# Fetching the odd heads' rows of w_in through a second DMA queue, and two of its pieces earlier

## The chip, the cores and the metric

The kernel runs on one core of a Trainium2 chip. A core has TensorE (matmuls), VectorE, ScalarE and GpSimd (elementwise work), and SyncE, which here only issues DMAs. ScalarE can issue DMAs too; each of the two has a queue of its own. The engines run their instruction lists in order and wait for each other through semaphores. The metric is the time of one execution on the device in microseconds (us), as the median over runs.

## The reference

A DeltaNet attention block feeds a SiLU feed-forward block. q, k, v and the output are float32; the two weights arrive as 64-bit numbers.

```
# q, k, v: (4, 8, 768, 48) float32, beta: (4, 8, 768)
k_n = k / (norm(k) + 1e-6)
state = zeros(B, H, 48, 48)
for t in range(768):
    y[t]  = q[t] @ state
    v_old = state^T @ k_n[t]
    state = state + beta[t] * outer(k_n[t], v[t] - v_old)
x = y as (B*S, H*D) = (3072, 384)
h = x @ w_in                      # w_in (384, 2048)
out = (h * sigmoid(h)) @ w_out    # w_out (2048, 384)
```

## The kernel before

The sequence is cut into 6 chunks of 128 tokens; a chunk has 4 units, one per batch. For each chunk the recurrence is turned into matrix form: `turn` transposes k and q through TensorE (tile `pt`) and copies them to `kq`; `score` makes the masked products `pa` into `ap`; `block_out` and `block_in` carry the 32 x 32 diagonal blocks through a DRAM tile so that all of them lie side by side in `g`; `invert` inverts them by 30 rank-one steps on VectorE (lines 477 and 481, tiles `rank` and `x`) and writes the inverses to DRAM as `up` and `low` (line 492); `move` (line 502) reads them back as `xi` and `xe` (in chunk 0 `xe` lies in `sums_of_w[1]`). `solve` then does the substitution: `merge` joins the 32-blocks (tiles `py`, `px`, line 551), `inner` and `across` apply them to v (tile `pz`), `update` and `new` make the new state and the output, whose transpose is `xT`. `feed_forward` of a chunk (`hidden` with tile `phid`, then `project` or `combine`) is spread between the steps of the next chunk's attention.

Weights arrive as 64-bit numbers and are narrowed to float32 on the chip. w_in comes in 8 pieces of 256 columns (`fetch_w_in`), w_out in 8 pieces of two 128-row blocks (`fetch_w_out`). A raw piece is 768 KB. A raw piece of w_in lands over 128 partitions by four DMAs, listed in `ROWS` (line 150): even heads fill partitions 0 to 63 (48 rows and 16 rows), odd heads 64 to 127 (48 and 16). The raw pieces live in rooms that are free at the time: pieces 0 to 3 in w_out's own buffers, 4 to 6 in buffers of the tag `gT`, 7 in `sums_of_g`. `narrow` (line 157) is five elementwise steps per piece: two on ScalarE (165, 170), three on VectorE (167, 173, 177), one addition on GpSimd (181). `fill(n)` takes the next n of these steps from `queue`, in the order of the pieces, and puts them between the steps of the attention; `Piece.begin` issues a piece's first ScalarE step.

The order is written out by hand. `pin` chains the instructions of an engine in program order; `in_line` does it for DMAs. All DMAs are issued by SyncE. The framework gives DMAs eight semaphores in turn, so each DMA's issue waits until the eighth DMA before it has landed. Where the DMA in question is issued by an engine that computes too, the wait stands in that engine's list.

In chunk 0, which the change touches, the order is: k and q of chunk 0, w_in pieces 0 and 1, blocks out and in, k of chunk 1, w_in pieces 2 and 3, q of chunk 1, v of chunk 0 (lines 914 to 954), the inversion, w_in pieces 4 to 7 and w_out piece 0 (lines 965 to 967), w_out piece 1, and in the substitution w_out pieces 2, 3, 4 and 5. During the inversion's steps 3, 5, 7 and 9 the four units of chunk 1 are transposed (line 960). `busy` (line 273, tile `pw`) puts filler products on TensorE; 20 of them stand after step 18 of the inversion (line 962) and some between the substitution's steps (line 996).

Of the kernel before, what the change touches and what calls it, by code (L numbers as in the profile page):

```python
# [21 lines left out]
def kernel(  # L22
# [22 lines left out]
    nc = tc.nc  # L45
    B, H, S, D = q.shape
# [7 lines left out]
    W = 64  # L54
# [24 lines left out]
    def behind(later, earlier, how=NoSync):  # L79

        tc.add_manual_dep(
            later.ins, earlier.ins.name,
            mybir.DependencyInfo(how, mybir.DependencyReason.DATA), reason="order",
        )
# [3 lines left out]
    def pin(op):  # L88

        engine = op.ins.engine  # L90
        if engine in pins:
            behind(op, pins[engine])
        pins[engine] = op
        return op
# [3 lines left out]
    def in_line(dma):  # L98

        if line:  # L100
            behind(dma, line[-1])
        line.append(dma)
        return dma
# [11 lines left out]
    def packed(t):  # L115
        return t[:].rearrange("p a e w -> p (a e) w")[:, :, 0:D]

    def chunk_of(src, i):
        b, c = units[i]
        return src[b, :, c * C : (c + 1) * C, :].rearrange("h t d -> t h d")  # L120

    def load_k(i):
        if i < N:
            in_line(nc.sync.dma_start(out=packed(kbufs[i % NK]), in_=chunk_of(k, i)))

    def load_q(i):
        if i < N:
            in_line(nc.sync.dma_start(out=packed(zbufs[i % NZ]), in_=chunk_of(q, i)))

    def load_v(i):  # L130
        if i < N and i not in vfs:
            vfs[i] = load.tile([P, H, D], FP32, name="vf", bufs=4)
            in_line(nc.sync.dma_start(out=vfs[i][:], in_=chunk_of(v, i)))
# [9 lines left out]
    for load_one in (load_k, load_q):  # L143
        for i in range(B):
            load_one(i)
    w_in = const.tile([P, NKT, DFF], FP32, name="w_in")
    HFF = NFF // 2
# [1 line left out]

    ROWS = [  # L150
        (at, lambda a, e=e, n=n: (2 * a + e) * D if n == D else (6 + e) * D + a * (W - D), n)
        for e in range(2)
        for at, n in ((W * e, D), (W * e + D, W - D))
    ]
    w_outs = [const.tile([P, HFF, DM], FP32, name=f"w_out{i}") for i in range(2)]

    def narrow(to, raw):

        low, high = raw[..., 0], raw[..., 1]
        bits = to.bitcast(U32)
        pin(nc.scalar.activation(out=to, in_=high.bitcast(FP32), func=ACTF.Abs))
        yield
        yield pin(nc.vector.tensor_scalar(
            out=to, in0=to, scalar1=LOW_HIGH, scalar2=None, op0=ALU.max
        ))
        pin(nc.scalar.activation(  # L170
            out=low.bitcast(I32), in_=low, func=ACTF.Identity, scale=2.0**-29, bias=plus23[:]
        ))
        yield pin(nc.vector.tensor_scalar(
            out=bits, in0=bits, scalar1=3, scalar2=0x3FFFFFFF,
            op0=ALU.logical_shift_left, op1=ALU.bitwise_and,
        ))
        done = pin(nc.vector.scalar_tensor_tensor(
            out=bits, in0=high, scalar=0xC0000000, in1=bits,
            op0=ALU.bitwise_and, op1=ALU.bitwise_or,
        ))  # L180
        adds.append(pin(nc.gpsimd.tensor_tensor(  # L181
            out=to.bitcast(I32), in0=to.bitcast(I32), in1=low.bitcast(I32), op=ALU.add
        )))
        yield done
# [5 lines left out]
    WF = GT  # L190
    NWI = DFF // WF
# [3 lines left out]
    def room(i, k):  # L195
        flat = w_outs[i][:].rearrange("p f m -> p (f m)").bitcast(U32)
        return flat[:, k * SIZE : (k + 1) * SIZE]

    def fetch_w_in(i):
        if i < 4:  # L200
            raw = room(1 - i // 2, i % 2)
        elif i < NWI - 1:
            raw = mlp.tile([P, SIZE], U32, name="raw", tag="gT", bufs=3)[:]
        else:
            raw = spare
        raw = raw.rearrange("p (a f) -> p a f", a=NKT)
        for at, row, rows in ROWS:
            step = row(1) - row(0)
            src = moe_w_in[row(0) : row(0) + rows, i * WF : (i + 1) * WF].bitcast(U32)
            pitch = src.ap[0][0]  # L210
            src = bass.AP(
                tensor=src.tensor, offset=src.offset,
                ap=[[pitch, rows], [pitch * step, NKT], [1, 2 * WF]],
            )
            in_line(nc.sync.dma_start(out=raw[at : at + rows], in_=src))
        raws[i] = raw.rearrange("p a (f j) -> p a f j", j=2)

    raws = {}

    sums_of_g = const.tile([P, 2, NFF // 2, C], FP32, name="sums_of_g")  # L220
    spare = sums_of_g[:].rearrange("p k f t -> p (k f t)").bitcast(U32)[:, 0:SIZE]
# [2 lines left out]
    sums_of_w = [const.tile([P, NFF // 2, HM], FP32, name=f"sums_of_w{i}") for i in range(3)]  # L224

    def narrow_w_in(i):
        return narrow(w_in[:, :, i * WF : (i + 1) * WF], raws.pop(i))

    places = {}

    def fetch_w_out(i):
        if i in (0, 1, 5):
            raw = room(1, min(i, 1))
        elif i in (4, 7):
            raw = sums_of_w[2 if i == 4 else 0][:].rearrange("p f m -> p (f m)").bitcast(U32)
        elif i == 6:
            raw = spare
        else:
            k = int(i == 3)
            if k not in places:  # L240
                places[k] = work.tile([P, SIZE], U32, name="raw_out", tag="ap", bufs=4)
            raw = places[k][:]
        raw = raw.rearrange("p (a f) -> p a f", a=2)
        src = moe_w_out.rearrange("(a p) f -> p a f", p=P)[:, 2 * i : 2 * i + 2, :].bitcast(U32)
        in_line(nc.sync.dma_start(out=raw, in_=src))
        raws[i] = raw.rearrange("p a (f j) -> p a f j", j=2)

    def narrow_w_out(i):
        at = 2 * i % HFF
        return narrow(w_outs[2 * i // HFF][:, at : at + 2, :], raws.pop(i))  # L250


    ident = const.tile([P, P], FP32, name="ident")
# [3 lines left out]
    for t in bkbufs:  # L257
# [4 lines left out]
        out=above[:], in_=above[:], pattern=[[1, P]], compare_op=ALU.is_gt, fill=0.0,  # L262
# [25 lines left out]
    def beta_of(c):  # L288
        pb = bank(psA, "a", "pb")
        pin(nc.tensor.transpose(pb[:, 0:BH], beta_fm[:, c * C : (c + 1) * C], ident[0:BH, 0:BH]))  # L290
        pin(nc.scalar.activation(out=beta_tok[:, c, :], in_=pb[:, 0:BH], func=ACTF.Copy))
# [51 lines left out]
    sizes, steps = {}, {}  # L343
# [524 lines left out]
                yield from project(c, b, o)  # L868


    A, CC, M = (psA, "a"), (psC, "c"), (psM, "m")

    def go(steps, n=1):
# [39 lines left out]
        scale(b)  # L913
    for i in range(B, 2 * B):
        load_k(i)
    fetch_w_in(2)
    fetch_w_in(3)
    for i in range(B, 2 * B):
        load_q(i)
    queue, narrowed = deque(), []  # L920

    class Piece:
        def __init__(self, name, steps):
            self.name, self.steps, self.begun, self.done = name, steps, False, 0

        def begin(self):
            if not self.begun:
                next(self.steps)
                self.begun = True

    def fill(n):

        ops = []
        while len(ops) < n and queue:
            piece = queue[0]
            piece.begin()

            if len(queue) > 1 and piece.done >= 2 and piece.name != ("out", 5):
                queue[1].begin()
            ops.append(next(piece.steps))  # L940
            piece.done += 1
            if piece.done == 3:
                narrowed.append(piece.name)
                queue.popleft()
        return ops


    queue.extend(Piece(("in", i), narrow_w_in(i)) for i in range(2))
    fill(5)
    for _ in range(4):  # L950
        busy()

    for i in range(B):
        load_v(i)
    next_us = []
    for n, done in enumerate(invert(0)):
        if n == 1:
            for c in range(1, NCH):
                beta_of(c)
        if n in (3, 5, 7, 9):  # L960
            next_us.append(list(turn(B + len(next_us), M, M))[0])
        if n == 18:
            for i in range(20):
                busy(done if i == 0 else None, Sync)
    for i in range(4, NWI):
        fetch_w_in(i)
    fetch_w_out(0)
    squares(1)
    norms(1)
    queue.extend(Piece(("in", i), narrow_w_in(i)) for i in range(2, NWI))  # L970
    queue.append(Piece(("out", 0), narrow_w_out(0)))

    def until(piece):
        while piece is not None and piece not in narrowed:
            fill(1)
# [1 line left out]
    def more(i, behind=None):  # L977

        until(behind)
        fetch_w_out(i)  # L980
        queue.append(Piece(("out", i), narrow_w_out(i)))

    fill(3)
    for b in range(B):
        size(b)
    more(1, ("in", 1))
    pieces = feed_forward(0)
    for n, _ in enumerate(solve(0, us)):
        fill(2)
        if n == 3:  # L990
            more(2)
            more(3)
            more(4)
        if n == 8:
            more(5, ("out", 1))
        for _ in range((3, 3, 2, 2, 1, 1, 1)[n] if n < 7 else 0):
            busy()
        if n >= 7:
            go(pieces, 2)
# [35 lines left out]
    for c in range(1, NCH):  # L1035
        if c + 1 < NCH:
# [7 lines left out]
            n = 0  # L1044
# [46 lines left out]
```

## Time and profile before

| what | us |
|---|---|
| median of 3 runs | 770.54 (770.52 to 770.78) |
| the profiled execution | 770.21 |
| its span | 768.5 |
| TensorE busy | 730.4 (95% of the span) |
| VectorE busy | 411.8 (54%) |
| ScalarE busy | 233.3 (30%) |
| GpSimd busy | 83.6 (11%) |
| DMA queue q1, share of 16 engines | 31.1% |

The span reaches from the first to the last instruction. Rows of the profile name an engine (PE is TensorE, PEld its weight loads, DVE VectorE, ACT ScalarE, POOL GpSimd, SP SyncE, SPq what SyncE issues), a line of the kernel, an operation, and output<-input. Where the page cuts the span in 40 slices, one slice is 19.2 us and a digit is the busy share in tenths. The chain that ended last is followed back from the last instruction; each of its rows gives a start, a duration and what was running or being waited for. A row "issue" is time in which the engine waited for nothing that the profile shows. DMA rows at SPq give the time of issuing, not of moving.

### The profile page before, as it was taken

To read this page: it belongs to the slowest core of one execution; us is meant where nothing else is said; L and a number is where in the kernel's file an instruction comes from. 1 tells how busy PE (TensorE), PEld (TensorE's weight loads), DVE (VectorE), ACT (ScalarE), POOL (GpSimd) and SP (SyncE) were. 2 spreads that over 40 slices of the span, in tenths; PEclk is the share of its full clock that TensorE was granted. 3 is DMA by queue.
4 is the path that set the end of the run, shared out by engine and by line. 5 is a ranking of instruction groups with operands and counts; after the bars stand their busy time and mean duration, and the time that the engine had idled before them with its cause. 6 is when DMAs were issued, how large, how long until landed. Compare 5 with 4: busy or idle time off the path is not lost.

```text
span 768.5 us, 16585 instructions
## 1 busy us (share of the span) xinstructions
PE 730.4 (95%) x6806; PEld 630.0 (82%) x6806; DVE 411.8 (54%) x1050; ACT 233.3 (30%) x512; POOL 83.6 (11%) x95
## 2 busy tenths in 40 slices
PE   7549799899999999999999999999999999999997
PEld 5336587478777999997999997999998999999987
DVE  4886678892336672445672445672445682221212
ACT  4524465311325212315212315212315212312020
POOL 4005246300003000002000002000002000000000
PEclk8859999999999999999999999999999999999999
DMA  9798847212025213034113044113043013010000
GB/s 164 116 167 162 172 146 194 52 66 42 13 54 106 42 48 70 6 77 101 33 49 69 5 77 96 38 49 70 5 77 77 15 49 70 5 30 0 21 1 21
DMA packets 155067, 50.93 MB, mean 66 GB/s; under 512 B 142544, under 2 KB 147536, under 8 KB 154992
## 3 DMA queue, kind: packets, MB, share of 16 engines
q1 hardware_dynamic: 154992, 49.87, 31.1%
q8 instruction: 54, 0.88, 0.5%
q14 instruction: 21, 0.17, 0.1%
HBM read 34.70 MB, written 14.16 MB: 64 GB/s over the span
## 4 chain that ended last, share of the span: by engine, by line
PE 88%; DVE 4%; DMA 3%; SPq 2%; issue 1%; ACT 1%; POOL 1%; ACTq 0%; DVEq 0%
PE phid L719 31%; PE px L813 14%; PE py L813 11%; PE pa L399 6%; PE pz L583 4%; PE pt L376 3%; PE po L742 3%; PE pw L276 3%; PE pyc L642 3%; PE pyc L614 2%; PE ph L567 2%; DMA z<-in_q_dram 2%; PE px L551 2%; PE py L551 2%; PE pu L625 2%; DVE x L481 1%
## 5 line engine op out<-in xcount | busy, mean ns | idle before, releaser
L719 PE MATMUL phid<-xT,w_in 128*128 128x256 f32 x1152 | 260.7, 382 | 2.2 <-ACT gT L729 1.6
L719 PEld LDWEIGHTS phid<-xT,w_in 128*128 128x128 f32 x1152 | 214.8, 190 | 37.2 <-issue 6.3
L729 ACT ACTIVATE gT<-phid 128x512 f32<-128x512 f32 x96 | 57.3, 598 | 189.6 <-PE phid L719 149.2
L415 DVE SCALAR_TENSOR_TENSOR ap<-pa,g,above 128x128 f32<-128x128 f32 x192 | 58.2, 376 | 43.7 <-ACT ap L409 43.7
L481 DVE TENSOR_TENSOR x<-x,rank 128x30 f32<-128x30 f32 (+9 forms) x180 | 59.6, 331 | 7.4 <-ACT x L470 1.1
L477 DVE TENSOR_TENSOR rank<-g,x 128x30 f32<-128x30 f32 (+9 forms) x180 | 59.4, 330 | 5.0
L795 DVE TENSOR_TENSOR sums_of_g<-gT 128x384 f32<-128x384 f32 (+1 forms) x60 | 29.2, 509 | 57.9 <-ACT gT L729 47.3
L813 PE MATMUL py<-w_out,sums_of_g 128*128 128x192 f32 x320 | 56.8, 329 | 0.0
L813 PE MATMUL px<-sums_of_w,sums_of_g 128*128 128x192 f32 x320 | 56.8, 329 | 0.0
L813 PEld LDWEIGHTS px<-sums_of_w,sums_of_g 128*128 128x128 f32 x320 | 52.2, 190 | 1.4 <-issue 1.4
L813 PEld LDWEIGHTS py<-w_out,sums_of_g 128*128 128x128 f32 x320 | 52.2, 190 | 0.4
L409 ACT ACTIVATE ap<-pa,g 128x128 f32<-128x128 f32 x144 | 41.6, 365 | 32.2 <-PE pa L399 32.2
L399 PE MATMUL pa<-kq 48*128 48x256 f32 x384 | 51.0, 401 | 0.2 <-DVE ap L415 0.2
L742 PE MATMUL po<-w_out,gT 128*128 128x384 f32 x128 | 44.7, 495 | 2.9 <-POOL w_out L181 2.9
L399 PEld LDWEIGHTS pa<-kq 48*128 48x128 f32 x384 | 36.9, 192 | 12.1 <-issue 8.1
L583 PEld LDWEIGHTS pz<-vf,xi 64*64 64x64 f32 x768 | 37.3, 138 | 8.5 <-issue 7.3
L583 PE MATMUL pz<-vf,xi 64*64 64x48 f32 x768 | 41.8, 224 | 0.4 <-ACT raw L170 0.3
L601 ACT COPY z<-pz 64x384 f32<-64x384 f32 x48 | 22.7, 474 | 60.8 <-PE pz L583 54.7
L438 POOL MEMSET x<- 128x1024 f32 x6 | 5.7, 950 | 313.5 <-PE pz L583 251.2
L574 DVE TENSOR_TENSOR vf<-vf,ph 128x384 f32<-128x384 f32 x20 | 11.1, 554 | 53.2 <-PE ph L567 53.2
L742 PEld LDWEIGHTS po<-w_out,gT 128*128 128x128 f32 x128 | 23.3, 190 | 18.4 <-POOL w_out L181 4.2
L574 DVE TENSOR_TENSOR vf<-vf,pz 64x384 f32<-64x384 f32 x24 | 13.4, 557 | 42.8 <-PE pz L591 26.0
(132 smaller groups left out, 924.1 us busy)
## 6 DMA issues: line engine op xcount, KB each, us to landing
kb<-in_k_dram SPq DMA_DIRECT2D x24, 192.0 KB, 3.1
z<-in_q_dram SPq DMA_DIRECT2D x24, 192.0 KB, 3.5
vf<-in_v_dram SPq DMA_DIRECT2D x24, 192.0 KB, 3.9
out_dram<-o SPq DMA_DIRECT2D x24, 192.0 KB, 2.0
blocks<-ap SPq DMA_DIRECT2D x96, 32.0 KB, 1.7
g<-blocks SPq DMA_DIRECT2D x24, 128.0 KB, 2.5
up<-x SPq DMA_DIRECT2D x6, 512.0 KB, 2.6
low<-g SPq DMA_DIRECT2D x6, 512.0 KB, 2.9
```

The costliest lines, as they stand in the source:

```text
L399: u["last"] = pin(nc.tensor.matmul(pa[e][:, pp * 2 * C : (pp + 1) * 2 * C], lhsT=kq[rows, 2 * g + pp, 0, :], rhs=kq[rows, 2 * g + pp, :, : ...
L409: copied = pin(nc.scalar.activation(out=ap[:, h, 0, :], in_=pa[e][:, at : at + C], func=ACTF.Copy, scale=bt[:, h : h + 1],))
L415: masked = pin(nc.vector.scalar_tensor_tensor(out=ap[:, h, j:2, :], in0=pa[e][:, at + j * C : at + 2 * C].rearrange("p (j t) -> p j t", j= ...
L477: pin(nc.vector.tensor_tensor(out=tv, in0=g[:, 0:m, m : m + 1].to_broadcast([P, m, n]), in1=x[:, m : m + 1, m + 1 : T].to_broadcast([P, m, ...
L481: yield pin(nc.vector.tensor_tensor(out=x[:, 0:m, m + 1 : T], in0=x[:, 0:m, m + 1 : T], in1=tv, op=ALU.add))
L551: pin(nc.tensor.matmul(pm[to, at : at + T], lhsT=left, rhs=right, start=True, stop=True))
L583: yield pin(nc.tensor.matmul(pzs[x][rows, h, :], lhsT=xis[x // HB][rows, x % HB * H + h, :], rhs=vs[x][rows, h, :], start=True, stop=True,))
L719: pin(nc.tensor.matmul(ph[:, j * GT : (j + 1) * GT], lhsT=w_in[:, a, (2 * f + j) * P : (2 * f + j + 1) * P], rhs=xTs[c, hf][:, a, :], star ...
L729: pin(nc.scalar.activation(out=gTs[f // FG][:, f % FG, :], in_=ph[:], func=ACTF.Silu, scale=0.5))
L742: pin(nc.tensor.matmul(po[:, 0:DM], lhsT=gTs[f // 2 // FG][:, f // 2 % FG, at : at + C], rhs=w_outs[f // HFF][:, f % HFF, :], start=(f == ...
L795: pin(nc.vector.tensor_tensor(out=sums_of_g[:, k, fs], in0=of[0], in1=of[1], op=op))
L813: pin(nc.tensor.matmul(to, lhsT=at, rhs=quarter(f, *b) if isinstance(b, tuple) else sums_of_w[b][:, f], start=start and f == 0, stop=f == ...
```

## The change

Three things change, all in chunk 0. The DMAs for the odd heads' rows of w_in's pieces 2 to 7 are issued by ScalarE, at their place in ScalarE's list; the even heads' stay with SyncE. `ROWS` is reordered so that the even and the odd part of 48 rows come first, then the two of 16. And the fetches move: q of chunk 1 goes ahead of pieces 2 and 3, piece 4 follows them, then v of chunk 0 (all in the inversion's steps 1 and 3), piece 5 is fetched in step 10; pieces 6 and 7 are fetched when the narrowing of pieces 4 and 5 begins; w_out's piece 0 goes out in the substitution's first step, ahead of pieces 6 and 7, and pieces 1, 4, 2, 3 in its fourth. The transposes of chunk 1 move from steps 3, 5, 7, 9 to 5, 7, 9, 11. The lists of TensorE, VectorE and GpSimd keep their order; ScalarE's gets 12 DMA issues more: six before the first copy of chunk 1's transposes, two before the copies of the fourth unit, two before each of the two copies of `xi` (line 556) in the substitution.

```diff
     ROWS = [
         (at, lambda a, e=e, n=n: (2 * a + e) * D if n == D else (6 + e) * D + a * (W - D), n)
-        for e in range(2)
-        for at, n in ((W * e, D), (W * e + D, W - D))
+        for n, off in ((D, 0), (W - D, D))
+        for e, at in enumerate((off, W + off))
     ]
...
-            in_line(nc.sync.dma_start(out=raw[at : at + rows], in_=src))
-        raws[i] = raw.rearrange("p a (f j) -> p a f j", j=2)
+            if at < W or i < ONE:
+                in_line(nc.sync.dma_start(out=raw[at : at + rows], in_=src))
+            else:
+                in_line(pin(nc.scalar.dma_start(out=raw[at : at + rows], in_=src)))
+        raws["in", i] = raw.rearrange("p a (f j) -> p a f j", j=2)
 
     raws = {}
+    ONE = 2
...
+    ORDER, TURN, OUT = {1: ("q", 2, 3), 3: (4, "v"), 10: (5,)}, (5, 7, 9, 11), {0: (0,), 3: (1, 4, 2, 3)}
...
-    fetch_w_in(2)
-    fetch_w_in(3)
-    for i in range(B, 2 * B):
-        load_q(i)
     queue, narrowed = deque(), []
 
     class Piece:
-        def __init__(self, name, steps):
-            self.name, self.steps, self.begun, self.done = name, steps, False, 0
+        def __init__(self, *name):
+            self.name, self.steps, self.done = name, None, 0
 
         def begin(self):
-            if not self.begun:
+            if self.steps is None:
+                kind, i = self.name
+                self.steps = (narrow_w_in if kind == "in" else narrow_w_out)(i)
                 next(self.steps)
-                self.begun = True
+                if kind == "in" and i in later:
+                    fetch_w_in(later[i])
+
+    later = {4: 6, 5: 7}
...
-    queue.extend(Piece(("in", i), narrow_w_in(i)) for i in range(2))
+    queue.extend(Piece(kind, i) for kind in ("in", "out") for i in range(NWI))
     fill(5)
...
-    for i in range(B):
-        load_v(i)
     next_us = []
     for n, done in enumerate(invert(0)):
...
-        if n in (3, 5, 7, 9):
+        for of in ORDER.get(n, ()):
+            if of == "q":
+                for i in range(B, 2 * B):
+                    load_q(i)
+            elif of == "v":
+                for i in range(B):
+                    load_v(i)
+            else:
+                fetch_w_in(of)
+        if n in TURN:
             next_us.append(list(turn(B + len(next_us), M, M))[0])
...
-    for i in range(4, NWI):
-        fetch_w_in(i)
-    fetch_w_out(0)
...
-    queue.extend(Piece(("in", i), narrow_w_in(i)) for i in range(2, NWI))
-    queue.append(Piece(("out", 0), narrow_w_out(0)))
...
-    more(1, ("in", 1))
     pieces = feed_forward(0)
     for n, _ in enumerate(solve(0, us)):
         fill(2)
-        if n == 3:
-            more(2)
-            more(3)
-            more(4)
+        for i in OUT.get(n, ()):
+            more(i, ("in", 1) if i == 1 else None)
         if n == 8:
             more(5, ("out", 1))
```

More of the change, by code (lines that the diff above doesn't have):

```diff
@@ L226, in narrow_w_in @@
     def narrow_w_in(i):
-        return narrow(w_in[:, :, i * WF : (i + 1) * WF], raws.pop(i))
+        return narrow(w_in[:, :, i * WF : (i + 1) * WF], raws.pop(("in", i)))
     places = {}
@@ L245, in fetch_w_out @@
         in_line(nc.sync.dma_start(out=raw, in_=src))
-        raws[i] = raw.rearrange("p a (f j) -> p a f j", j=2)
+        raws["out", i] = raw.rearrange("p a (f j) -> p a f j", j=2)
     def narrow_w_out(i):
         at = 2 * i % HFF
-        return narrow(w_outs[2 * i // HFF][:, at : at + 2, :], raws.pop(i))
+        return narrow(w_outs[2 * i // HFF][:, at : at + 2, :], raws.pop(("out", i)))
     ident = const.tile([P, P], FP32, name="ident")
@@ L980, in more @@
         fetch_w_out(i)
-        queue.append(Piece(("out", i), narrow_w_out(i)))
     fill(3)
```

## The prediction

> **What bounds the kernel now.** I read the page's 40 slices first, then the chain that ended last. The span is 768.5 us; the profiled execution took 770.21 us, the median of the runs is 770.54, so 1.71 us of that execution lie outside the span and the median is 0.33 above it. Sums below are made against 770.21 and carried to the median by adding 0.33. About 0.2% (1.5 us) is what a measurement of this kernel can tell from no change.
>
> ```profile
> PE   7549799899999999999999999999999999999997
> DMA  9798847212025213034113044113043013010000
> ```
>
> TensorE is full from slice 7 (134 us) on, and the change moves no instruction of TensorE, VectorE or GpSimd in their program orders. So whatever happens happens before some 130 us, in the slices where the DMA row is high, and what is won or lost there shifts the rest as it stands. The chain in that stretch:
>
> ```profile
> 34.40 5.92 DMA w_out<-in_moe_w_in_dram
> 40.34 8.54 DMA z<-in_q_dram
> 48.92 6.20 PE pt L376 x28
> 55.12 12.90 PE pw L276 x40
> 68.03 1.13 PE py L551 x64
> ...
> 79.72 0.93 PE px L551 x50
> 80.65 3.02 issue
> 83.67 0.43 PE px L551 x14
> ```
>
> Pieces 2 and 3 of w_in (34.40, in w_out's buffers) hold up q's loads, q holds up the transposes pt, these hold up 20 filler products pw (12.90 us, in program order before the substitution), and the substitution's first product py starts at 68.03. Later TensorE stands 3.02 us in the middle of a run of px for nothing but "issue". Next, SyncE's queue in order of time:
>
> ```profile
> 34.40 4.24 SPq L215 DMA_DIRECT2D w_out<-in_moe_w_in_dram  x8
> 40.34 7.92 SPq L128 DMA_DIRECT2D z<-in_q_dram  x4
> 48.30 4.64 SPq L133 DMA_DIRECT2D vf<-in_v_dram  x4
> 56.02 0.34 SPq L492 DMA_DIRECT2D up<-x  x1
> 57.16 0.34 SPq L492 DMA_DIRECT2D low<-g  x1
> 60.37 0.85 SPq L502 DMA_DIRECT2D sums_of_w<-low  x2
> ...
> 66.57 8.36 SPq L215 DMA_DIRECT2D raw<-in_moe_w_in_dram  x12
> ```
>
> py needs the inverse's blocks: up and low, then sums_of_w from low. These are issued at 60.37 and 60.8 and land, by the 2.5 us of the DMA list, at 63.3. So py was free to start 4.7 us before it did. Last, busy time by stretch:
>
> ```profile
> 35.00:49.00 14.00, 0.86 (x5) 0.46 (x4) 12.73 (x36) 0.59 (x1) 0.00 (x0) 0.50 1.21 166
> 49.00:56.00 7.00, 7.00 (x32) 5.62 (x33) 6.28 (x22) 4.05 (x7) 0.00 (x0) 0.60 1.24 164
> 68.00:80.00 12.00, 12.00 (x251) 8.05 (x252) 7.93 (x10) 6.38 (x10) 6.46 (x6) 1.00 1.06 175
> ```
>
> The last two figures are the DMA share and GB/s: the DMA engines are full from 35 to 56 at 165 GB/s. up goes out just as that backlog is gone. Anything put ahead of it delays it.
>
> **What the skill says.** "SBUF — State Buffer", section on the DMA port swizzle: partitions 0 to 63 reach only 8 of 16 ports, and 64 partitions measured 196 GB/s at 1 MiB against 328 for 128. The trace agrees: w_in's pieces, written half by half, move about 169 GB/s (82 packets of 2 KB per us, 193 ns each in the median, though the first hundred of a burst take 84 ns), and w_out's, over 128 partitions, about 400 (3 KB packets of 121 ns). Its next section says two concurrent DMAs, one on each half, gained only 6%. "DMA: Bandwidth & Descriptors", on issuing engines: DMAs of SyncE and ScalarE run on the same 16 engines. On queues and rings: each engine takes turns between its rings. No run here shows either, as all loads use one queue.
>
> **The change part by part.**
>
> *q first.* z0 is issued at 34.4 instead of 40.34, behind four k loads only. A load of 192 KB takes some 1.1 us of the DMA engines (768 KB in the 4.64 us of vf's issues), so the four q land between 40 and 45. This removes most of the 13 us that TensorE waited. The copies of the transposes are ScalarE's, however, and six DMA issues now stand before them there. Each DMA waits for the landing of the eighth before it (one of eight counters in turn), so the third and fourth odd-row issues wait for z1 and z3: ScalarE is free at 44.5 + 3 x 0.6 = 46.3. Each transpose and copy takes 0.9 (48.92 to 55.12 for seven). Six copies end by 52, the last transpose by 53. pw needs also step 18 of the inversion, over at 47.6. So pw runs 53 to 66 instead of 55.1 to 68.0: at most 2 us for py. Piece 5's two issues on ScalarE wait for piece 4's odd rows (about 51 to 54); behind them queue two copies (1.2) and g's copy for low (1.1), which was made at 56.03. Taken at nothing: the inversion, over at 55.94, covers them; past 54 each us is one us for low.
>
> *Pieces 4 and 5 ahead of up.* 1.57 MB more, 9.3 us at 169 GB/s. If pieces on two queues write both halves at once, all four go faster. Bounds: 1.06 times (the skill's 6%), and 2 times (84 ns packets, 16 ports). I take 1.3: the engines take turns between the halves, but still collide on ports, as 48 rows load them unevenly. Four pieces then take 18.6 / 1.3 = 14.3 us instead of 9.3 for two: 5.0 more. From that I take 1 us (0 to 3), an estimate, as the odd rows also run beside q's and v's short packets. The blocks land at 63.3 + 4.0 = 67.3, after pw's end at 66. py: -0.7 us.
>
> *Less traffic in the substitution.* Pieces 4 and 5 no longer follow at 66.57, so ScalarE's two waits on raw (1.5 us, at 74.76 and 79.73) go; they were hidden by TensorE's own work. The 3.02 us gap lies under these fetches; a 16 KB record of the instruction queue ends with it, and the same products in later stretches with a quiet DMA show no gap above 0.4. I take it for an instruction fetch held up by the backlog: 0 to -3.0. Pieces 6 and 7 and the first w_out piece still fall near it, so I take -2.2.
>
> *Four issues on ScalarE there.* 4 x 0.55 (SyncE's own 4.24 / 8), none waiting for anything late. The first pair stands before xi's copy, which followed the narrowing by 0.05: 1.1 less the 0.7 that ScalarE waited for raw: +0.4 (0 to 1.2). The second pair falls where px is still running. Named at nothing: the new row order of pieces 0 and 1 (landed 4 us before use), w_out's piece order (needed from 99 us, and bound by GpSimd's reads).
>
> Sum: -0.7 - 2.2 + 0.4 = -2.5; 770.21 - 2.5 = 767.7, carried to the median 768.0.
>
> **Rivals.**
> 1. *The backlog wins; slower.* Two queues give 1.06 times: 17.5 us, 8.2 more, 0.5 hidden: blocks at 71.0, py +3.0. The gap moves along with the late fetches (-0.3), +0.4: 773.6. For it: the skill, and a DMA share already above 1.2. Against: fast packets at a burst's start, so reading is not the limit. It decides where the shift of py passes 1.8: blocks 6.5 later, four pieces above 16.8 us, under 1.11 times or 187 GB/s.
> 2. *Full gain.* Pieces at 1.6 times or more: py follows pw at 65.8 (-2.2), the gap goes whole (-3.0): 765.3.
> 3. *A wash.* py +0.8, half the gap, +0.4: 770.2. That is also the case in which the second queue only reorders the traffic.
> 4. *ScalarE held.* Piece 4's odd rows land at 57: two copies and g's end at 60.5, low 3.4 late: 773.9. ScalarE's wait then shows on DMA. Against: the odd rows start before the even ones, which queue behind q.
>
> **How the numbers follow.** Chances: forecast 0.38, rival 2 0.17, rival 3 0.15, rival 1 0.25, rival 4 0.05. Faster: rival 2 and nearly all of the forecast, 0.53; same: rival 3 and a rest, 0.17; slower: rivals 1 and 4, 0.30. The range reaches from rival 2 with half a us more to just short of rival 1: 764.8 to 773.2; the forecast's own is 766 to 769.5.
>
> **What would show it.** z0 lands near 40, pt starts near 47, pw near 53. The time from pw's end to py is the verdict on rate: 1 us by the forecast, none by rival 2, 5 by rival 1. The DMA column from 40 to 60 should rise from 165 to about 200 GB/s, with a second queue in the list. The 3.02 us gap should shrink. ScalarE's waits should name no DMA beyond 1 us between 48 and 57. The forecast fails if up or low waits for anything but VectorE and ScalarE past 60, or if the stretch after 130 us changes its length.

## The result and the profile after

The changed kernel's median is 773.29 us over 14 runs (770.88 to 776.95), that of the kernel before beside it 771.31 us (769.82 to 774.62). The ratio is 1.0015, with a 95% interval of 0.9998 to 1.0032: 1.2 us more, give or take 1.3, so neither a gain nor a loss is shown (the two medians stand 2.0 us apart). The forecast was 768.0. The profiled execution is the slowest of the 14 (776.95 us, span 775.0), so its trace holds more than the median does, and the two have to be told apart.

The page first: the DMA row of the slices and the queues.

```profile
PE   7557899899999999999999999999999999999997
DMA  9798927303025204026203025213024013010000
...
q1 hardware_dynamic: 153648, 47.51, 29.6%
q10 hardware_dynamic: 1344, 2.36, 1.9%
```

The second queue is there, with 2.36 MB. TensorE is nearly full from slice 7 on, as before. Next the chain that ended last (start, duration, what ran or was waited for):

```profile
62.32 0.35 SPq L496
62.79 5.98 DMA low<-g
68.79 0.32 SPq L506
69.16 2.19 DMA sums_of_w<-low
71.40 1.91 PE py L555 x62
73.30 4.14 PE pw L280 x6
77.44 1.68 PE py L555 x64
...
86.42 0.93 PE px L555 x50
87.35 0.96 issue
88.31 0.43 PE px L555 x14
```

Before, filler products led straight into py at 68.03. Now the chain runs through the inverse's blocks: low takes 5.98 us to land, sums_of_w lands at 71.35, and py starts at 71.40. The first 62 products of py take 1.91 us where 64 took 1.13, and six pw take 4.14 in place of 2.13. The gap in px is 0.96 in place of 3.02. In the same view of before six pw and the first phid stand so:

```profile
69.16 2.13 PE pw L276 x6
98.67 2.86 PE phid L719 x12
```

And the first phid of the changed kernel:

```profile
105.58 2.86 PE phid L723 x12
```

SyncE's queue shows what up and low wait for:

```profile
34.39 6.72 SPq L128 DMA_DIRECT2D z<-in_q_dram  x4
41.15 3.52 SPq L216 DMA_DIRECT2D w_out<-in_moe_w_in_dram  x4
48.37 0.89 SPq L216 DMA_DIRECT2D raw<-in_moe_w_in_dram  x2
50.76 7.56 SPq L133 DMA_DIRECT2D vf<-in_v_dram  x4
58.37 3.82 SPq L216 DMA_DIRECT2D raw<-in_moe_w_in_dram  x2
62.32 0.35 SPq L496 DMA_DIRECT2D up<-x  x1
62.79 0.36 SPq L496 DMA_DIRECT2D low<-g  x1
```

up stood at 56.02 before and stands at 62.32 now, behind v and the even rows of piece 5, whose two issues alone take 3.82 us. ScalarE's list, and busy time by the stretches of the prediction (PE, PEld, DVE, ACT, POOL, then TensorE's clock, DMA share, GB/s):

```profile
36.15 10.64 ACTq L218 DMA_DIRECT2D w_out<-in_moe_w_in_dram  x4
46.83 0.92 ACTq L218 DMA_DIRECT2D raw<-in_moe_w_in_dram  x2
47.85 0.58 ACT L387 COPY kq<-pt 128x512 f32<-128x512 f32 x1 [12.50 <-issue]
```

```profile
35.00:49.00 14.00, 2.79 (x13) 1.94 (x12) 12.69 (x37) 1.39 (x4) 0.00 (x0) 0.50 1.32 161
49.00:56.00 7.00, 6.77 (x32) 4.97 (x31) 6.31 (x21) 2.27 (x4) 0.00 (x0) 0.82 1.08 175
68.00:80.00 12.00, 8.91 (x137) 6.12 (x138) 2.48 (x4) 2.27 (x4) 5.53 (x5) 0.57 0.64 140
```

Six issues hold ScalarE until 47.75. The rate is 161 and 175 GB/s where it was 166 and 164: with two queues no more was moved than with one. And the clock of the last stretch is 0.57 where it was 1.00.

What this makes of the time: py 71.40 - 68.03 = 3.4 later, the gap 3.02 - 0.96 = 2.1 shorter, 1.3 in all. The runs' ratio gives 1.2, but its interval is too wide for that to be a test. The first phid, though, comes at 105.58 in place of 98.67, 6.9 later, and the span is 6.5 longer. By subtraction 5.6 us are left, and I put them down to the clock: TensorE ran at 0.5 from 68.5 to 78.8 and from 89.0 to 99.2, 20.5 us, where the execution shown of before had 3.4 (85.4 to 88.8).

One thing limits such differences between two profiles. The inversion, whose work nothing here changes, ends at 55.94 before, at 56.35 in the changed kernel and at 54.1 to 57.8 in the experiments. So 0.4 of the 3.4 us stood there before py's turn came, and below times of two profiles are counted from the inversion's end too where it matters.

### The profile page after: what moved, and what is told of

Its sections match the earlier page's. It is cut to its first block, busy times and chain, and to the rows that moved or that the text cites. A ratio compares the mean times of both kernels' runs of the same rounds, so it can differ in the third digit from the quotient of the medians.

```text
span 775.0 us, 16579 instructions
## 1 busy us (share of the span) xinstructions
PE 735.7 (95%) x6806; PEld 633.3 (82%) x6806; DVE 409.9 (53%) x1050; ACT 232.4 (30%) x512; POOL 83.7 (11%) x95
## 3 DMA queue, kind: packets, MB, share of 16 engines
q10 hardware_dynamic: 1344, 2.36, 1.9%
## 4 chain that ended last, share of the span: by engine, by line
PE 85%; DMA 5%; DVE 3%; SPq 3%; ACT 1%; POOL 1%; issue 1%; DVEq 0%; ACTq 0%
PE phid L723 31%; PE px L817 14%; PE py L817 10%; PE pa L403 5%; PE pz L587 4%; PE po L746 3%; PE pyc L646 3%; PE pyc L618 2%; PE ph L571 2%; PE pt L380 2%; PE py L555 2%; PE pw L280 2%; PE px L555 2%; DMA z<-in_q_dram 2%; PE pu L629 2%; DVE x L485 1%
## 5 line engine op out<-in xcount | busy, mean ns | idle before, releaser
L799 DVE TENSOR_TENSOR sums_of_g<-gT 128x384 f32<-128x384 f32 (+1 forms) x60 | 29.3, 510 | 57.8 <-ACT gT L733 47.1
L280 PE MATMUL pw<-state,ident 128*128 128x384 f32 x80 | 33.8, 572 | 4.0 <-DVE state L140 2.8
```

What stands on the lines that cost most here:

```text
L280: done = pin(nc.tensor.matmul(pw[:, 0:DM], lhsT=ident[:], rhs=states[B - 1][:].rearrange("p a w -> p (a w)")[:, 0:DM], start=True, stop=Tr ...
```

## The experiments

The theory after the result is this: the bytes ahead of up make the blocks late, a second queue adds no rate, and TensorE's wait ahead of py costs clock on top. Its rivals are ScalarE held by its issues, the new place of q, and the clock as chance. Ratios are to the kernel before, run beside each.

**All rows on SyncE, the changed order kept.**

```diff
-            if at < W or i < ONE:
+            if True:
```

> The changed kernel with all rows issued by SyncE again; the order of the fetches stays as changed. Theory (what sets the time is the 1.57 MB put ahead of up; a second queue moves no more bytes per us): w_in's pieces move at 165 to 175 GB/s as with two queues, the inverse's blocks (sums_of_w from low) land within 1.5 us of the changed kernel's 71.4, py starts there, and the time is the changed kernel's within 2 us (771.5 to 775). ScalarE is not held, so the transposes end by 48 instead of 53 and TensorE idles longer before py, which can cost clock. Rival A (ScalarE's held issues are what costs): 2 us or more faster than the changed kernel. Rival B (two queues did help the rate): blocks 3 us or more later than 71.4, 776 or more.

Measured: 771.56 us, ratio 0.9993 (0.9976 to 1.0011). TensorE in order of time:

```profile
48.23 14.86 PE L280 MATMUL pw<-state,ident 128*128 128x384 f32 x40 [2.23 <-DVE x L485]
69.45 0.31 PE L555 MATMUL py<-sums_of_w,ap 32*32 32x32 f32 x2 [6.36 <-DMA sums_of_w<-low]
70.65 1.91 PE L555 MATMUL py<-sums_of_w,ap 32*32 32x32 f32 x62 [0.90 <-DMA sums_of_w<-low]
```

With ScalarE free the fillers start at 48.23, five us earlier than in the changed kernel (53.18), and it is all lost in the wait: py stands at 70.65, 0.75 us earlier. 36 to 54 us move 165 to 183 GB/s, against 160 to 172. So the hold on ScalarE was hidden but for 0.75 us at most, and the blocks' lateness needs no second queue.

**Each piece as one DMA over 128 partitions.** Same bytes, same 2 KB rows; the rows are taken in consecutive order, so the sorting of w_in's rows by heads is left out.

```diff
-        for at, row, rows in ROWS:
...
-                ap=[[pitch, rows], [pitch * step, NKT], [1, 2 * WF]],
...
+        src = moe_w_in[0:P, i * WF : (i + 1) * WF].bitcast(U32)
...
+            ap=[[pitch, P], [pitch * P, NKT], [1, 2 * WF]],
...
+        in_line(nc.sync.dma_start(out=raw, in_=src))
```

> The changed kernel with each piece of w_in fetched by one DMA over 128 partitions from 128 consecutive rows per third, on SyncE; left out is the sorting of the rows by heads, so the products see w_in's rows in another order. The bytes, the 2 KB rows and their pitch in memory stay. Theory (the rate is set by how many ports a DMA's partitions reach): a piece moves at 300 GB/s or more, packets of 2 KB take 80 to 120 ns, the blocks land by 64, py follows pw at 61 to 64, and the time is 4 to 8 us below before, 762.5 to 766.5. Rival (the rate is set by reading 2 KB rows 16 KB apart): still 165 to 185 GB/s, blocks near 71, 771 to 776.

Measured: 764.78 us, ratio 0.9911 (0.9889 to 0.9932). Busy time by stretch:

```profile
42.00:48.00 6.00, 5.65 (x27) 4.40 (x25) 5.52 (x15) 3.51 (x7) 0.00 (x0) 0.57 1.20 294
48.00:54.00 6.00, 4.45 (x14) 2.73 (x15) 5.48 (x16) 0.51 (x2) 0.00 (x0) 1.00 1.10 282
```

The same stretches of the changed kernel:

```profile
42.00:48.00 6.00, 0.00 (x0) 0.00 (x0) 5.55 (x14) 0.15 (x1) 0.00 (x0) 0.50 1.26 162
48.00:54.00 6.00, 5.28 (x27) 4.33 (x28) 5.45 (x17) 3.21 (x6) 0.00 (x0) 0.71 1.07 172
```

It is 294 and 282 GB/s in place of 162 and 172, and a packet of 2 KB takes 84 ns in the median between 30 and 100 us, where it takes 202 in the changed kernel. The reading of 2 KB rows and the queue are not the limit; the form in which a piece is written is. The run changes two things of that form at once, 128 partitions in place of 48 or 16 and one DMA in place of four, and does not tell them apart. That the partitions decide agrees with the Trainium skill, "SBUF — State Buffer", section on the DMA port swizzle. A later section there, on two DMAs for the two halves, gives 6% for two at once; here no gain can be told.

**Eight more calls of the filler, and eight fewer** (28 as shown, and 12).

```diff
-            for i in range(20):
+            for i in range(28):
                 busy(done if i == 0 else None, Sync)
```

> The changed kernel with 28 instead of 20 filler products before the substitution (8 x 0.65 = 5.2 us of TensorE work where it idled from 66.2 to 71.4). Theory (the idle stretch lets the granted clock drop to half, and the substitution then runs its first products at half speed): the clock stays at 1.0 from 55 on, py still starts near 71.4, the stretch from py to the first phid shrinks from 34.2 us to 30 to 32; 2 to 4 us faster than the changed kernel's profiled span of 775.0, median 769.5 to 772. Rival (the clock is chance and the fillers only work): same as the changed kernel or slower by up to 1 us.

> The changed kernel with 12 calls of the filler in place of 20 (5.2 us less), so TensorE stands idle for some 10 us ahead of py at 71 in place of 5. Theory (idle ahead of py brings the half clock): stretches at 0.5 of at least 10 us follow, begun earlier, and the time is 774 to 777, 1 to 3 us over the changed kernel's 773.3. Rival (the clock is set by something else): the stretches stand where they stood or fall away, and the time is within 1 us of the changed kernel.

Measured with 28: 771.74 us, ratio 1.0014 (0.9991 to 1.0036). With 12: 776.45 us, ratio 1.0069 (1.0049 to 1.0089). The chain with 28, then TensorE in order of time with 12:

```profile
51.58 18.06 PE pw L280 x56
69.64 1.13 PE py L555 x64
```

```profile
67.82 0.31 PE L555 MATMUL py<-sums_of_w,ap 32*32 32x32 f32 x2 [8.51 <-DMA sums_of_w<-low]
68.86 1.91 PE L555 MATMUL py<-sums_of_w,ap 32*32 32x32 f32 x62 [0.74 <-DMA sums_of_w<-low]
```

With 28 TensorE never stands ahead of py, no stretch at 0.5 follows and py takes 1.13. With 12 it stands for over nine us (59.3 to 68.9, but for two products), the clock is 0.5 from 64.4 to 74.6, and py takes 1.91. So the wait ahead of py brings the clock down: with 12 the mean clock of the runs is 0.971 in the median, against 0.976 with 20 and 0.980 with 28. The forecast for 12 held. Of that for 28 the clock in the trace and the median came out, but the ratio, 1.0014 beside 1.0015 with 20, shows no gain. Both profiled executions are the fastest of their runs (14 with 28, 21 with 12), so a typical trace can look worse. With 28 the gap in px is gone as well.

**Pieces 4 and 5 behind up and low**, first with their odd rows still with ScalarE, then all on SyncE, then with those of pieces 2 and 3 alone with ScalarE.

```diff
-    ORDER = {1: ("q", 2, 3), 3: (4, "v"), 10: (5,)}
+    ORDER = {1: ("q", 2, 3), 3: ("v",), 10: ()}
...
+    fetch_w_in(4)
+    fetch_w_in(5)
     squares(1)
```

> The changed kernel with w_in's pieces 4 and 5 fetched after the inverse's blocks again; q first, two queues and the rest stay. Theory (the bytes ahead of up are what delays py): blocks land at 63 to 64.5, py starts at pw's end, 65 to 66.5, no idle, no loss of clock before py; the substitution runs under the traffic of pieces 4 to 7 as before, with a gap of about 3 us; 1 to 3 us faster than before, 767.5 to 770. Rival (the second queue itself or ScalarE's issues cost): same as before or slower, 770.5 to 774.

> The changed kernel with all rows on SyncE's queue and pieces 4 and 5 issued behind up and low. Theory (the place of pieces 4 and 5 made the blocks late): up is issued at 54 to 56 us and low by 57, sums_of_w lands at 61.5 to 63.5 in place of 71.4, py starts at 62 to 64.5, and, as no issue stands in ScalarE's list, the 5 us hold on the xi moves does not appear: 765 to 769. Rival (ScalarE's issues alone, not the place, had made the earlier trial of this late): as the theory. Rival (pieces 6 and 7 behind narrowing bring the loss): no better than the one-queue form with pieces 4 and 5 early, 771 to 772.

> The form with pieces 4 and 5 behind up and low (one queue: 771.7), with the odd heads' rows of pieces 2 and 3 alone fetched through ScalarE's queue. Theory (a second queue raises no rate): 32 to 56 us move the same bytes per us within 5%, py starts within 1.5 us of the one-queue form's 61.98, and the time is within 1.5 us of it, 770.2 to 773.2; ScalarE's four issues hold its copies of kq until some 47, which puts the fillers 1 to 4 us later but not more. Rival (two queues do raise the rate when they do not carry pieces 4 and 5 as well): pieces 2 and 3 land 2 us or more earlier and v and up with them.

Measured: 780.07 us, ratio 1.0113 (1.0075 to 1.0150); 771.72 us, 1.0004 (0.9982 to 1.0026); 770.94 us, 0.9987 (0.9973 to 1.0002). The first was a miss, and ScalarE's list shows why:

```profile
63.70 8.06 ACTq L218 DMA_DIRECT2D raw<-in_moe_w_in_dram  x4
71.86 1.76 ACT L310 ACTIVATE z<-kb 128x384 f32<-128x384 f32 x4 [16.02 <-DMA raw<-in_moe_w_in_dram]
```

The issues queued for landings of earlier DMAs, and the squares behind them, which norms and v's scaling need, came 8 us late. A held issue costs what waits behind it: next to nothing in the changed kernel, 8 us here. With all rows on SyncE, py starts at 61.98, as forecast: the place of pieces 4 and 5 had made the blocks late.

```profile
61.98 0.24 PE L555 MATMUL py<-sums_of_w,ap 32*32 32x32 f32 x2
76.78 1.10 PE L587 MATMUL pz<-vf,xi 64*64 64x48 f32 x16 [4.11 <-issue]
```

But the time did not follow: 771.72, where 765 to 769 was expected, and TensorE now stands 4.11 us ahead of pz. The third run, against the second, shows what the second queue does to pieces 2 and 3: 158 to 184 GB/s from 36 to 54 us where one queue had 166 to 172, and a time within a us. py stands at 63.70, 1.7 later (2.7 from the inversion's end) where at most 1.5 was expected: ScalarE's hold puts the fillers' start to 50.70, and here they, not the blocks, come last.

**q first alone**, in the kernel before, with 20 and with 24 fillers. This is where the missing gain was found.

```diff
-    fetch_w_in(2)
-    fetch_w_in(3)
     for i in range(B, 2 * B):
         load_q(i)
+    fetch_w_in(2)
+    fetch_w_in(3)
```

> The kernel before with the second half's q loads issued ahead of pieces 2 and 3, all on SyncE's queue; nothing else moved, pieces 4 to 7 stay behind up and low. Theory (blocks wait for bytes, not for q): up is still issued at 55 to 57 us and sums_of_w still lands at 62.5 to 64, because the same bytes stand ahead of them; but z now lands by 41, the last transpose leaves TensorE by 48, the fillers run 47.6 to 60.5, and py starts when the blocks land, at 63 to 64.5 in place of 68.03: 3 to 4.5 us earlier, so 767 to 769 if the clock holds. The clock rival: the 2.5 to 4 us that TensorE now stands idle ahead of py bring a stretch at 0.5 as in the changed kernel, which takes 1 to 3 us back: 769 to 772. Rival, q not on the path: fillers and py stay where they were, within 0.5 us, and the time is that of before.

> The same with 24 calls of the filler in place of 20 (2.6 us more at 0.645 us a call). Theory: the fillers now end at 63 or so, with the blocks; py starts at 63 to 64.5; no stretch at 0.5 follows; 766 to 769, and no slower than with 20. If the clock is not set by the idle ahead of py, a stretch at 0.5 follows all the same.

Measured: 768.86 us, ratio 0.9985 (0.9958 to 1.0013); with 24, 771.82 us, 1.0007 (0.9983 to 1.0032). With 24 the fillers ran till 65.6, and py at 65.65 and the time missed what was expected; the four more were too many. In the run with 20, py starts at 62.92, 5.1 us earlier than before (5.4 from the inversion's end), but the substitution is no earlier at pz: 78.00, where it was 77.17. TensorE, then ScalarE:

```profile
62.92 1.57 PE L551 MATMUL py<-sums_of_w,ap 32*32 32x32 f32 x64
72.44 1.56 PE L276 MATMUL pw<-state,ident 128*128 128x384 f32 x4
78.00 1.10 PE L583 MATMUL pz<-vf,xi 64*64 64x48 f32 x16 [4.01 <-issue]
```

```profile
69.89 1.02 ACT L170 ACTIVATE w_out<-w_out,plus 128x768 int32<-128x768 uint32 x1
76.42 0.89 ACT L165 ACTIVATE w_in<-raw 128x768 f32<-128x768 f32 x1 [5.51 <-DMA raw<-in_moe_w_in_dram]
77.33 0.57 ACT L556 COPY xi<-px 32x512 f32<-32x512 f32 x1
```

px was there at 72.4. Its copy to xi stands in ScalarE's list behind the narrowing of piece 4, which waits for piece 4's landing at 76.4. TensorE's row says "issue", and only ScalarE's list tells what it is. In the kernel before the same narrowing waited 0.68 us and started at 74.76:

```profile
74.76 0.92 ACT L165 ACTIVATE w_in<-raw 128x768 f32<-128x768 f32 x1 [0.68 <-DMA raw<-in_moe_w_in_dram]
```

There px and piece 4 were due almost together. Fetched early, pieces 4 and 5 make the blocks late; fetched late, they hold xi.

**The narrowing moved behind the first pz copies**, with q first, then in the kernel before, then with q first and the steps spread: 2, 1, 0, 1, 2, 3, 3, 4.

```diff
     for n, _ in enumerate(solve(0, us)):
-        fill(2)
+        fill((2, 1, 0, 0, 3, 4)[n] if n < 6 else 2 + (n < 8))
```

> The kernel before with q first on SyncE's queue, and the narrowing of piece 4 and what follows it moved behind the first pz copies in ScalarE's list (fewer filling steps in the first four steps of the substitution, more in the next ones). In the run with q alone first, py stood at 62.92 us, but pz waited till 78.00 because the copy of xi stood in ScalarE's list behind piece 4's narrowing, which waited 5.5 us for piece 4's landing at 76.4. Theory (piece 4's landing, through ScalarE's list, is the next bound): pz starts at 74 to 74.5, px of the second half at 77.5 to 78.5, the first phid at 93 to 95 in place of 96.98; 764 to 767.5. Rival (the 4 us ahead of pz is TensorE's instruction fetch, as the gap in px of before): the gap stays, pz at 77 to 78, the time that of q alone first, 768 to 769.5. Rival (the narrowings moved later now hold phid): phid no earlier than 97 with waits on narrowing, 769 to 773.

> The kernel before with only the narrowing of piece 4 and what follows moved behind the first pz copies, q in its old place. Theory: before's profile shows ScalarE waiting 0.68 us for piece 4 ahead of the copy of xi, and TensorE has no wait ahead of pz, so at most 1 us is won there; the 3.02 us gap in px stays or moves: 769 to 771.5. Rival (the narrowing between the products costs more than its waits): 766 to 768.

> q first on one queue, the narrowing later but spread: filling steps 2, 1, 0, 1, 2, 3, 3, 4 over the first eight steps of the substitution, where the run before had 2, 1, 0, 0, 3, 4, 3, 3. Piece 4's first narrowing now stands ahead of the second copy of xi, behind the first pz copies. Theory (only the copy of xi must not wait for piece 4's landing; VectorE crowded with narrowing at 81 to 86 us cost the other form a part): pz at 74 to 76 as there, fewer and shorter issue gaps between 82 and 88, first phid at 94.5 to 97.5; 765 to 767.5. Rival (the first narrowing still waits for its landing at 76.4 to 77 and holds the second copy of xi): px of the second half's copy no earlier than in the form with q alone first, 768 to 769.5.

Measured: 766.77 us, ratio 0.9918 (0.9897 to 0.9939); 771.18 us, 0.9978 (0.9964 to 0.9992); 766.10 us, 0.9939 (0.9914 to 0.9964). The chain of the last:

```profile
65.60 1.36 PE py L551 x64
66.96 2.13 PE pw L276 x6
69.09 1.13 PE px L551 x64
70.22 1.49 PE pw L276 x4
71.71 1.06 PE pz L583 x16
...
81.83 2.15 issue
...
92.57 2.86 PE phid L719 x12
```

pz follows at once, at 71.71, and the first phid comes at 92.57, 6.1 us earlier than in the kernel before (98.67); 1.4 of that stood at the inversion's end already, 4.7 are left, and the profiled execution is the fastest of its 13. Both came earlier than expected. In the first of the three pz came at 75.69, not the 74 to 74.5 expected (sums_of_w landed late and the clock was 0.5 from 69.8 to 73.2), and its first phid at 97.77, outside the forecast; its time was inside, and its profiled execution is the slowest of its six. The second run shows the later narrowing alone: 0.2%, with its time inside the forecast. So q first shows 0.15% alone, which is not told from nothing, the later narrowing 0.2%, and both together 0.6 to 0.8%. Either form with both beats the kernel before, on one queue, and by the ratios the changed kernel too, which was not run beside them; which of the two is better was not told apart.

## Why the prediction was wrong, by its own steps

- *q first.* Right in its parts: ScalarE was to be free at 46.3 and was at 47.75, pw was to run from 53 to 66 and ran from 53.18 to 66.25. What it left out is the next limit in line. Alone, q first moved py by 5.1 us and the time by 0.15% (interval across 0), because xi's copy sat behind piece 4.
- *Pieces 4 and 5 ahead of up.* **This is the step that failed.** It took 1.3 times for the rate of two queues; the runs showed 160 to 172 GB/s with two queues against 165 to 183 with one. Its condition, both halves written at once, was rarely met either: ScalarE's queue had 2 KB packets in flight for 22.6 us between 30 and 100, and SyncE's had them at the same time for 6.4 of these only. Where each had four or more in flight, 3.8 us in all, 155 GB/s were moved, against 177 and 184 with one of the two alone (with pieces 2 and 3 alone on two queues: 189, against 176 and 187). With no gain in rate, pieces 4 and 5 push up from 56.02 to 62.32 and sums_of_w to 71.35. Rival 1 had the blocks at 71.0. The argument against it, fast packets at a burst's start, told only that reading was not the limit; the run with 128 partitions and one DMA a piece showed that the form of the writing was. The prediction's figure for 40 to 60 us was misread too: 165 GB/s is that of 35 to 56; from 40 to 60 the kernel before moves 184, and the changed one 169 instead of the 200 expected. up waited in SyncE's queue till 62.32, a sign of failure that the prediction had named.
- *py.* Forecast -0.7, measured +3.4 (+3.0 from the inversion's end). The mark the prediction set, the time from pw's end to py, was 1 us by the forecast and 5 by rival 1; it was 5.15.
- *Less traffic in the substitution.* Forecast -2.2, measured -2.1. That the number came out is luck as far as the runs show. With 28 fillers the gap in px was 0 under the same fetches, in the kernel before with the later narrowing it was 0.73 under before's fetches, and in the last run 2.15 us of "issue" stand elsewhere. So the fetches of pieces 4 and 5 are not shown to make it. The instruction fetch itself has more for it: a 16 KB record of the instruction queue ends 1.3 to 1.6 us before the end of such a gap in all seven traces that have one (82.22 and 83.67 before, where the prediction took the two ends for one; 86.72 and 88.31 in the changed kernel; 82.62 and 83.98 in the last run). No run tested it.
- *Four issues on ScalarE in the substitution, and the rest at nothing.* No wait of theirs on the path. Rival 4, low held by ScalarE, did not come: low waited in SyncE's queue.
- *The sum.* -2.5 forecast; +3.4 - 2.1 = +1.3 by the trace without the clock, 1.2 by the ratio. Rival 1's place and cause with a size between rivals 3 and 1, since the gap shrank all the same. That rival 1's 773.6 lies beside the measured 773.29 is luck: the kernel before measured 771.31 beside it, 0.8 above the value that the sums started from. Two rivals' sums don't keep the prediction's own terms: rival 2's 765.3 leaves out the +0.4, and rival 4's 773.9 is the median before plus the whole 3.4, without the 4.7 us that py had to spare.
- *Not in any case:* the clock. 10.2 us at 0.5 came with the wait ahead of py in the profiled execution; the other 10.2, from 89.0 on, follow only the 0.96 us gap, and what brought them is not shown. Together they are some 5.6 us there. The median carries little of it: the changed kernel's runs have a mean clock of 0.976, those of before 0.975 beside the first experiments. A line through those 44 runs of before gives 0.54 us of span for each 0.001 of mean clock; at 0.978, such lines put the span of before at 768.1 to 769.3 in four batches and that of the changed kernel at 770.1.

## What to carry to other kernels

Here a second DMA queue added no rate to transfers that each wrote half the partitions. Before splitting transfers over queues, see whether their form is what limits them; count bytes over the measured rate, and put what the critical chain needs ahead of them. When a wait is taken away, look in the program order of every engine on the way for the next instruction that waits for a transfer: a copy of half a us behind a narrowing for a late piece ate a gain of five. And before explaining a median with a profiled difference, take off what stood there before the change could act, and split the rest into schedule and clock.

## What the runs showed of the hardware

- TensorE standing for a few us was followed by half clock, in stretches of 3.413 us or a multiple of it. Waits of 3.0 to 4.1 us (before, the two runs of q first alone, and the last two with pieces 4 and 5 late) were followed by a stretch of 3.4; waits of 5.1, 6.4 and 8.5 us by 10.2. But waits of only 2.1 to 2.9 us were followed by 6.8 in three runs (pieces 4 and 5 late, all on SyncE and with two pieces on two queues, and q first with the later narrowing) and by 3.4 in the last run, so the length of the wait does not settle that of the stretch. It began within some 2 us of the wait's end, or in the wait. In the kernel before with the later narrowing, 10.2 us followed a wait of 0.73. That waiting is the cause is shown for the stretch ahead of py by the two filler counts; what decides the length is not.
- Half clock near the start goes with a late start of all that follows. In seven of the 14 traces TensorE ran at 0.5 for 6.8 us (in one 10.2) from some 10 us on; k of chunk 1 was issued at 31.3 to 33.4 us in these, and at 29.5 to 30.6 in the other seven. That the clock makes the difference is not shown.
- A DMA issue in a compute engine's list held the whole list: 10.64 us for four issues in the changed kernel, 8.06 in another form, while earlier transfers landed.
- The same 2 KB rows took 84 ns a packet with one DMA over 128 partitions and 202 with four over halves.
